# A gated attention and a two-layer network in one kernel: input loads issued six tiles ahead instead of three, and the output pieces of the layer taken one slot later

## The chip, the cores and the metric

The kernel runs on one core of a Trainium2 chip. The metric is device time in microseconds (us) of one launch, the median of several runs. The engines work side by side, each through its own list of instructions in order, and wait for each other by semaphores: PE (TensorE, matrix multiply, with PEld for its weight loads), DVE (VectorE), ACT (ScalarE), POOL (GpSimd) and SP (SyncE, which here only issues DMA transfers).

## The reference

The input is `q`, `k`, `v`, `f_logit`, each of shape (4, 8, 768, 48) in float32, and three weight matrices.

```python
f = 1.0 / (1.0 + np.exp(-f_logit))
for t in range(S):
    state = f[:, :, t, :, None] * state + np.einsum('bhd,bhe->bhde', k[:, :, t], v[:, :, t])
    y[:, :, t] = np.einsum('bhd,bhde->bhe', q[:, :, t], state)
x = y.transpose(0, 2, 1, 3).reshape(B * S, H * D)      # 3072 x 384
out = np.maximum(x @ w1, x @ w2) @ w_out               # d_ff = 1024
```

## The kernel before

The 768 steps of a sequence are cut into 6 chunks of 128, which with the batch of 4 makes 24 tiles of 128 time steps and all 8 heads. Tile n is chunk n // 4 of batch n % 4. Inside a tile the recurrence is done by matrix products, and a small state per batch goes from chunk to chunk. Two tiles make a group g of 256 tokens, for which the layer is computed: the maximum is split as x·w2 + relu(x·(w1 − w2)), so that the layer consists of "d" pieces (the relu part, `piece_d`, four to a group) and "o" pieces (`piece_o`, two to a group, 11 matmuls each, which sum both parts into 128 output rows).

All instructions of an engine stand in the order in which the program's code is run (`manual_schedule`). After a start, in which the weights are loaded and prepared, the loop at the end of the function turns once for each tile; one turn, n, is called slot n here. Its steps stand in this order on every engine they use:

- `load(n + 3)`: four DMAs on SP's queue, for `ft`, `kt`, `qt`, `vt`, 192 KB each, each into one of `bufs=6` buffers of its name.
- A(n): on PE the matmuls into `at_e` and `at_o`, on DVE their masks `at_m`. A slot is taken to begin where PE begins A(n).
- Y(n − 1): on PE `y` and `sadd`, on ACT the copy of `y` into `xT`, on DVE and POOL the new state. Where n is even, ACT also issues two DMAs of 24 KB (`xT<-xT`), which put part of the group's activations into other partitions; the first d piece of the group, in slot n + 1, needs them.
- C(n + 2): on PE `cum`, on ACT the three exponentials `f_inv`, `f_dec`, `f_last`.
- M(n + 2): on POOL `kp` and `qp`.
- one d piece: six matmuls into `h` on PE, one relu into `gT` on ACT.
- V(n + 1) and T(n + 1): on DVE `vb`, on PE transposes into `trp`, on DVE their copy `trs`.
- one d piece.
- E(n + 3): on ACT `tmp_e` from `ft` and then `ell`, which C of the next slot needs.
- one o piece: 11 matmuls into `o` on PE, the copy `ob` on DVE, the store of `ob` on SP's queue.

So SP's queue holds loads and stores in one row, and a load behind a store is issued only when the store's `ob` has been written. Besides, each DMA of SP and of ACT has one of eight semaphores (`DMAHW0` to `DMAHW7`, handed out in turn over both queues), and is issued only when the DMA that had the same one before it has landed.

The pieces stand in one list. The d pieces of group g come into it in slot 2g + 3, and an o piece is not taken as long as a d piece of its group is left; the first o piece of a group follows, in slot 2g + 4, directly on the group's last d piece. The two o pieces of group 0 are there from the start, so slots 2 and 3 have one each, slots 4 and 5 have none, and from slot 6 each slot has one.

Of the kernel before, what the change touches and what calls it, by code (L numbers as in the profile page):

```python
# [16 lines left out]
def kernel(  # L17
# [25 lines left out]
    FG = d_ff // C  # L43
    KT = HD // C
    GB = 2
    NT = GB * C
    n_tiles = nch * B

    consts = ctx.enter_context(tc.tile_pool(name="consts", bufs=1))
    inp = ctx.enter_context(tc.tile_pool(name="inp", bufs=6))  # L50
    work = ctx.enter_context(tc.tile_pool(name="work", bufs=2))
    xpool = ctx.enter_context(tc.tile_pool(name="xpool", bufs=2))
    opool = ctx.enter_context(tc.tile_pool(name="opool", bufs=3))
# [13 lines left out]
    def load(n, names="fkqv"):  # L67
        c, b = divmod(n, B)
        for nm in names:
            t = inp.tile([C, H, D], F32, name=f"{nm}t", tag=f"{nm}t")  # L70
            nc.sync.dma_start(out=t, in_=sources[nm][b, :, c * C:(c + 1) * C, :].rearrange("h p d -> p h d"))  # L71
            loaded[n][nm] = t
# [262 lines left out]
            nc.vector.tensor_copy(m2[:, i, :], ps)  # L335


    AHEAD = 5
    done = set()
    steps = {  # L340
        "E": stage_E, "M": stage_M, "V": stage_V,
# [6 lines left out]
    def do(names, n):  # L348
        for nm in names:
            if 0 <= n < n_tiles and (nm, n) not in done:  # L350
                done.add((nm, n))
                steps[nm](n)
# [5 lines left out]
    load_weights()  # L358
    load(2, "kqv")
    load(3, "kqv")  # L360
    load(4)
    do("E", 0)
    do("E", 1)
    for n in range(2):
# [19 lines left out]
    do("M", 3)  # L384
    do("E", 4)

    queue = [("o", 0, b) for b in range(GB)]

    def next_piece(kind):
        for i, (kd, g, j) in enumerate(queue):  # L390
            if kd == kind:
                if kd == "o" and any(p[0] == "d" and p[1] == g for p in queue):
                    return
                queue.pop(i)
                (piece_d if kind == "d" else piece_o)(g, j)
                return

    n = 2
    while n < n_tiles + 2 or queue:
        if n % GB == 1 and 3 < n <= n_tiles + 1:  # L400
            g = (n - 3) // GB
            queue += [("d", g, fp) for fp in range(FG // 2)] + [("o", g, b) for b in range(GB)]
        if 5 <= n + 3 < n_tiles:
            load(n + 3)
        do("A", n)
        do("Y", n - 1)
        do("C", n + 2)
        do("M", n + 2)
        next_piece("d")
        do("V", n + 1)  # L410
        do("T", n + 1)
        next_piece("d")
        do("E", n + 3)
        next_piece("o")
        n += 1


# [28 lines left out]
```

## Time and profile before

| | us |
|---|---|
| median of 3 runs | 180.33 (179.46 to 181.15) |
| profiled execution, its own time | 179.95 |
| its span, first to last instruction | 178.1 |
| PE busy | 144.2 (81% of the span) |
| ACT busy | 95.4 (54%) |
| DVE busy | 88.8 (50%) |
| POOL busy | 64.1 (36%) |
| DMA queue of SP, share of the 16 engines' span | 76.1% |

The span is the time between the first and the last instruction in one profiled execution; 1.85 us of that execution lie around it. A busy engine need not be the one that everything waits for, since PE's share is an average over a start of some 50 us, in which it waits for weights, the loop, and the last slots.

### The profile page before, as it was taken

What the parts mean: (1) busy time and instruction counts of PE and PEld (TensorE: products, weight loads), DVE (VectorE), ACT (ScalarE), POOL (GpSimd) and SP (SyncE); (2) the same over time, 40 slices, a digit from 0 to 9 for tenths busy, and PEclk for the clock granted to TensorE, in tenths of its full rate; (3) what the DMA queues carried; (4) which work ended last, traced back from release to release, by engine and by line L of the source; (5) the groups of instructions that cost most, each with busy time, mean ns of one, the idle gap of its engine ahead of it and who ended that gap; (6) DMA issues with size and microseconds to landing.
All of it is one profiled execution on the core that took longest, in us unless ns stands there. A gap on an engine that the chain in (4) does not pass through costs nothing.

```text
span 178.1 us, 4161 instructions
## 1 busy us (share of the span) xinstructions
PE 144.2 (81%) x1636; PEld 97.6 (55%) x1637; DVE 88.8 (50%) x168; ACT 95.4 (54%) x205; POOL 64.1 (36%) x79
## 2 busy tenths in 40 slices
PE   0157361877979579999999999999999999999992
PEld 0034250353546457676776757677576775767661
DVE  8029149210289735554666555466554564551121
ACT  4263550385443564866568576684866748343520
POOL 2086009500035181455525445552455524300000
PEclk9999999996999957999999999999999999999999
DMA  6999999990006999689799997999999986111112
GB/s 121 190 228 403 391 261 184 199 157 0 0 4 142 230 196 168 124 172 223 164 225 174 203 186 155 218 188 216 175 189 217 190 167 153 44 53 50 55 48 90
DMA packets 106772, 29.18 MB, mean 164 GB/s; under 512 B 100736, under 2 KB 105984, under 8 KB 106752
## 3 DMA queue, kind: packets, MB, share of 16 engines
q1 hardware_dynamic: 105216, 28.32, 76.1%
q10 hardware_dynamic: 1536, 0.59, 1.3%
q8 instruction: 13, 0.21, 0.5%
q14 instruction: 7, 0.06, 0.1%
HBM read 23.59 MB, written 4.72 MB: 159 GB/s over the span
## 4 chain that ended last, share of the span: by engine, by line
PE 43%; DMA 27%; ACT 10%; DVE 7%; SPq 6%; ACTq 3%; issue 2%; DVEq 0%
DMA ft<-in_f_logit_dram 14%; PE h L275 12%; PE o L285 12%; DMA kt<-in_k_dram 5%; DMA xT<-xT 5%; SPq L71 5%; PE o L282 4%; DMA w_f<-in_moe_w_dram 3%; DVE wdn L305 3%; PE m2n L326 3%; ACTq L265 3%; PE trp L176 2%; PE wdp L312 2%; ACT tmp_e L136 2%; PE y L221 2%
## 5 line engine op out<-in xcount | busy, mean ns | idle before, releaser
L163 POOL TENSOR_TENSOR kp<-kt,f_inv 128x384 bf16<-128x384 f32 x24 | 25.8, 1076 | 51.1 <-ACT f_inv L156 41.0
L275 PE MATMUL h<-xT,wd 128*128 128x256 bf16 x288 | 39.5, 279 | 0.5 <-DMA xT<-xT 0.4
L285 PE MATMUL o<-wo,gT 128*128 128x384 bf16 x192 | 38.0, 327 | 0.5 <-ACT gT L277 0.2
L288 DVE COPY ob<-o 128x384 f32<-128x384 f32 x24 | 13.3, 556 | 45.3 <-PE o L285 41.0
L277 ACT ACTIVATE gT<-h 128x512 bf16<-128x512 f32 x48 | 27.9, 609 | 11.1 <-PE h L275 10.7
L275 PEld LDWEIGHTS <-wd 128*128 128x128 bf16 x288 | 26.4, 99 | 4.2 <-DMA xT<-xT 0.7
L285 PEld LDWEIGHTS <-gT 128*128 128x128 bf16 x192 | 17.3, 98 | 17.3 <-ACT gT L277 7.2
L165 POOL TENSOR_TENSOR qp<-qt,f_dec 128x384 bf16<-128x384 f32 x24 | 24.7, 1031 | 0.3 <-DMA qt<-in_q_dram 0.3
L184 DVE COPY trs<-trp 128x1024 bf16<-128x1024 bf16 x24 | 16.5, 689 | 14.6 <-PE trp L176 14.6
L251 POOL TENSOR_TENSOR state<-tmp_s,f_last 128x256 bf16<-128x256 f32 x16 | 10.6, 662 | 36.5 <-DVE tmp_s L250 36.5
L260 ACT CAST xT<-y 128x512 bf16<-128x512 f32 x24 | 13.9, 581 | 16.9 <-PE y L221 16.9
L136 ACT ACTIVATE tmp_e<-ft 128x384 f32<-128x384 f32 x24 | 12.7, 531 | 16.4 <-DMA ft<-in_f_logit_dram 16.4
L156 ACT ACTIVATE f_inv<-cum 128x384 f32<-128x384 f32 x24 | 11.8, 491 | 16.9 <-POOL state L251 8.4
L143 PE MATMUL cum<-ell,ut 128*128 128x384 bf16 x24 | 8.7, 363 | 11.8 <-ACT ell L137 11.5
L202 DVE TENSOR_TENSOR at_m<-at_e,ut 128x512 bf16<-128x512 f32 x24 | 16.4, 682 | 2.2 <-PE at_o L194 2.1
L202 DVE TENSOR_TENSOR at_m<-at_o,ut 128x512 bf16<-128x512 f32 x24 | 16.3, 680 | 0.0
L282 PE MATMUL o<-m,xT 128*128 128x384 bf16 x72 | 15.6, 326 | 0.0
L169 DVE CAST vb<-vt 128x384 bf16<-128x384 f32 x24 | 11.8, 492 | 2.5 <-DMA vt<-in_v_dram 2.5
L137 ACT ACTIVATE ell<-tmp_e 128x384 bf16<-128x384 f32 x24 | 12.6, 523 | 0.8
L146 PEld LDWEIGHTS <-ell 128*128 128x128 bf16 x96 | 6.1, 100 | 12.3 <-issue 10.9
L194 PE MATMUL at_e<-trs 48*128 48x128 bf16 x96 | 10.1, 229 | 3.2 <-DVE trs L184 3.2
L157 ACT ACTIVATE f_dec<-cum 128x384 f32<-128x384 f32 x24 | 11.7, 488 | 0.0
(51 smaller groups left out, 171.7 us busy)
## 6 DMA issues: line engine op xcount, KB each, us to landing
ft<-in_f_logit_dram SPq DMA_DIRECT2D x24, 192.0 KB, 3.9
kt<-in_k_dram SPq DMA_DIRECT2D x24, 192.0 KB, 4.3
qt<-in_q_dram SPq DMA_DIRECT2D x24, 192.0 KB, 4.2
vt<-in_v_dram SPq DMA_DIRECT2D x24, 192.0 KB, 4.3
out_dram<-ob SPq DMA_DIRECT2D x24, 192.0 KB, 2.4
w_f<-in_moe_w_dram SPq DMA_DIRECT2D x6, 512.0 KB, 6.1
wo_f<-in_moe_w_out_dram SPq DMA_DIRECT2D x2, 768.0 KB, 9.2
xT<-xT ACTq DMA_DIRECT2D x24, 24.0 KB, 3.7
```

The costliest lines, as they stand in the source:

```text
L136: nc.scalar.activation(tmp, ft, AF.Exp, bias=0.0, scale=-1.0)
L137: nc.scalar.activation(padded["ell"][n % NB][:, :, 0:D], tmp.rearrange("p (h d) -> p h d", h=H), AF.Ln, bias=1.0, scale=1.0)
L163: nc.gpsimd.tensor_mul(padded["kp"][n % NB][:, :, 0:D], loaded[n]["k"], f_inv.rearrange("p (h d) -> p h d", h=H))
L165: nc.gpsimd.tensor_mul(padded["qp"][n % NB][:, :, 0:D], loaded[n]["q"], f_dec.rearrange("p (h d) -> p h d", h=H))
L184: nc.vector.tensor_copy(t, ps)
L202: nc.vector.tensor_mul(m[:, r], ps[r], ut4)
L260: nc.scalar.copy(xT[g][:, :, b * C:(b + 1) * C], ys.pop(n))
L275: nc.tensor.matmul(out=ps[:, f, :], lhsT=wd[:, kt, ff * C:(ff + 1) * C], rhs=xT[g][:, kt, :], start=(kt == 0), stop=(kt == KT - 1))
L277: nc.scalar.activation(gT[g][:, 2 * fp:2 * fp + 2, :], ps, AF.Relu)
L282: nc.tensor.matmul(out=ps, lhsT=xT[g][:, kt, b * C:(b + 1) * C], rhs=m2[:, kt, :], start=(kt == 0), stop=False)
L285: nc.tensor.matmul(out=ps, lhsT=gT[g][:, ff, b * C:(b + 1) * C], rhs=wo[:, ff, :], start=False, stop=(ff == FG - 1))
L288: nc.vector.tensor_copy(ob, ps)
```

## The change

There are eight buffers of each input instead of six, `AHEAD` is 6 and is now used: tiles 4 to 7 are loaded before the loop instead of tile 4 alone, and slot n loads tile n + 6 instead of n + 3. The list of pieces becomes two, one for each kind, each entry with the slot from which it may be taken: d pieces of group g from slot 2g + 3 as before, o pieces from slot 2g + 5 instead of 2g + 4. The o pieces of group 0 keep slots 2 and 3.

```diff
-    inp = ctx.enter_context(tc.tile_pool(name="inp", bufs=6))
+    inp = ctx.enter_context(tc.tile_pool(name="inp", bufs=8))
...
-    AHEAD = 5
+    AHEAD = 6
...
-    load(4)
+    for n in range(4, 2 + AHEAD):
+        load(n)
...
-    queue = [("o", 0, b) for b in range(GB)]
-
-    def next_piece(kind):
-        for i, (kd, g, j) in enumerate(queue):
-            if kd == kind:
-                if kd == "o" and any(p[0] == "d" and p[1] == g for p in queue):
-                    return
-                queue.pop(i)
-                (piece_d if kind == "d" else piece_o)(g, j)
-                return
+    queue = {"d": [], "o": [(0, b, 0) for b in range(GB)]}
+
+    def next_piece(kind, slot):
+        if queue[kind] and queue[kind][0][2] <= slot:
+            g, j, _ = queue[kind].pop(0)
+            (piece_d if kind == "d" else piece_o)(g, j)
...
-            queue += [("d", g, fp) for fp in range(FG // 2)] + [("o", g, b) for b in range(GB)]
-        if 5 <= n + 3 < n_tiles:
-            load(n + 3)
+            queue["d"] += [(g, fp, n) for fp in range(FG // 2)]
+            queue["o"] += [(g, b, n + 2) for b in range(GB)]
+        if 2 + AHEAD <= n + AHEAD < n_tiles:
+            load(n + AHEAD)
```

On SP's queue, around the first store, the program before has the load of tile 5 (its last row here is `vt_522`), the store, the load of tile 6 and the second store. The semaphores that a row waits for stand in brackets.

```order
L71 DMA vt_522<-in_v_dram 128x8x48 [waits DMAHW1_49]
L291 DMA out_0_dram<-ob_578 128x384 [waits DMAHW2_49,DVE_49]
L71 DMA ft_581<-in_f_logit_dram 128x8x48 [waits DMAHW3_49,Activation_49]
L71 DMA kt_583<-in_k_dram 128x8x48 [waits DMAHW4_49,Pool_49]
L71 DMA qt_585<-in_q_dram 128x8x48 [waits DMAHW5_49,Pool_49]
L71 DMA vt_587<-in_v_dram 128x8x48 [waits DMAHW6_49]
L291 DMA out_0_dram<-ob_665 128x384 [waits DMAHW0_49,DVE_49]
```

At the same place of SP's queue the changed program has the end of tile 7's load (`vt_201`), all of tile 8's, the store, tile 9's load and the second store.

```order
L71 DMA vt_201<-in_v_dram 128x8x48 [waits DMAHW1_49]
L71 DMA ft_540<-in_f_logit_dram 128x8x48 [waits DMAHW4_49,Activation_49]
L71 DMA kt_542<-in_k_dram 128x8x48 [waits DMAHW5_49,Pool_49]
L71 DMA qt_544<-in_q_dram 128x8x48 [waits DMAHW6_49,Pool_49]
L71 DMA vt_546<-in_v_dram 128x8x48 [waits DMAHW7_49,DVE_49]
L291 DMA out_0_dram<-ob_602 128x384 [waits DMAHW0_49,DVE_49]
L71 DMA ft_605<-in_f_logit_dram 128x8x48 [waits DMAHW1_49,Activation_49]
L71 DMA kt_607<-in_k_dram 128x8x48 [waits DMAHW2_49,Pool_49]
L71 DMA qt_609<-in_q_dram 128x8x48 [waits DMAHW5_49,Pool_49]
L71 DMA vt_611<-in_v_dram 128x8x48 [waits DMAHW6_49]
L291 DMA out_0_dram<-ob_689 128x384 [waits DMAHW7_49,DVE_49]
```

Nine tiles instead of six stand ahead of the first store. `DMAHW2`, for which `kt_607` of tile 9 waits, was last given to the first `xT` DMA of group 1, which ACT issues in slot 4; so SP stops there until that transfer has landed. The later `xT` pairs stop SP in the same way, each once in every two slots, for instance the `vt` of tile 10 (group 2, slot 6), the `ft` of tile 13 (group 3, slot 8) and the fourth store (group 4, slot 10).

On DVE, in slots 5 and 6 (each row of `tmp_s`, `vb`, `trs` and the two of `at_m` is one tile's), the difference is:

```order
 L169 CAST vb_114<-vt 128x8x48
 L184 COPY trs<-trp 128x1024
-L288 COPY ob<-o 128x384
 L202 TENSOR_TENSOR at_m<-at_e,ut_118 128x512
 L202 TENSOR_TENSOR at_m<-at_o,ut_118 128x512
```

Slot 6 loses its o piece; on PE the 11 matmuls of the piece are gone from the same place. At the end of DVE's list the difference is:

```order
 L202 TENSOR_TENSOR at_m<-at_e,ut_118 128x512
 L202 TENSOR_TENSOR at_m<-at_o,ut_118 128x512
-L288 COPY ob<-o 128x384 x5
-L441 UNCONDITIONAL_BRANCH
+L288 COPY ob<-o 128x384 x6
+L439 UNCONDITIONAL_BRANCH
```

The piece stands at the end now, behind the last d pieces; in between, every slot has one o piece as before, but of the group before.

## Rows read from the trace of the kernel before

**Rows 1.** Who waited for whom: us in total, times, longest us.

```profile
ACT tmp_e L136 <- DMA ft<-in_f_logit_dram: 16.4, 13, 3.1
PEld L285 <- ACT gT L277: 7.2, 18, 0.6
```

**Rows 2.** The same for SP's queue.

```profile
SPq L291 <- DVE ob L288: 63.6, 23, 16.8
...
SPq L71 <- DMA xT<-xT: 7.6, 2, 7.1
```

**Rows 3.** Stretches: us, busy PE, PEld, DVE, ACT, POOL, PEclk, DMA share, GB/s.

```profile
62.50:68.50 6.00, 4.88 (x39) 3.40 (x40) 2.15 (x5) 3.62 (x9) 3.73 (x5) 0.50 1.18 185
74.00:148.00 74.00, 72.76 (x944) 50.90 (x944) 42.32 (x84) 48.15 (x111) 35.86 (x42) 1.00 0.95 189
```

**Rows 4.** PE in order of time, slots 4 to 7: start, us, what, [idle before].

```profile
57.65 0.41 PE L221 MATMUL y<-at_m,vb 128*64 128x128 bf16 x8
...
63.50 0.48 PE L143 MATMUL cum<-ell,ut 128*128 128x384 bf16 x1 [1.35 <-ACT ell L137]
...
64.18 1.46 PE L275 MATMUL h<-xT,wd 128*128 128x256 bf16 x6
...
67.70 0.28 PE L194 MATMUL at_e<-trs 48*128 48x128 bf16 x1
...
75.02 0.81 PE L275 MATMUL h<-xT,wd 128*128 128x256 bf16 x6
```

**Rows 5.** ACT in order of time, slots 3 and 4.

```profile
58.16 0.52 ACT L136 ACTIVATE tmp_e<-ft 128x384 f32<-128x384 f32 x1 [2.34 <-DMA ft<-in_f_logit_dram]
...
59.15 0.57 ACT L260 CAST xT<-y 128x512 bf16<-128x512 f32 x1
59.75 1.23 ACTq L265 DMA_DIRECT2D xT<-xT  x2
```

**Rows 6.** ACT in order of time in slot 10.

```profile
90.35 0.58 ACT L260 CAST xT<-y 128x512 bf16<-128x512 f32 x1 [0.28 <-PE y L221]
90.96 1.21 ACTq L265 DMA_DIRECT2D xT<-xT  x2
...
93.08 1.11 ACT L277 ACTIVATE gT<-h 128x512 bf16<-128x512 f32 x2
...
94.62 0.52 ACT L137 ACTIVATE ell<-tmp_e 128x384 bf16<-128x384 f32 x1
```

**Rows 7.** PE in order of time: slots 8, 9 and 10, and A of 22.

```profile
78.66 0.23 PE L194 MATMUL at_e<-trs 48*128 48x128 bf16 x1
...
84.17 0.23 PE L194 MATMUL at_e<-trs 48*128 48x128 bf16 x1
...
85.58 0.81 PE L275 MATMUL h<-xT,wd 128*128 128x256 bf16 x6
...
87.34 0.65 PE L282 MATMUL o<-m,xT 128*128 128x384 bf16 x3
87.83 1.46 PE L285 MATMUL o<-wo,gT 128*128 128x384 bf16 x8
89.22 0.23 PE L194 MATMUL at_e<-trs 48*128 48x128 bf16 x1
...
92.88 1.86 PE L285 MATMUL o<-wo,gT 128*128 128x384 bf16 x8
...
153.56 0.23 PE L194 MATMUL at_e<-trs 48*128 48x128 bf16 x1
```

**Rows 8.** The xT DMAs' time to landing: all 24, slots 8, 18 and 22.

```profile
DMA to landing us min/median/max: 1.9/3.7/5.8
...
DMA to landing us min/median/max: 3.1/3.3/3.5
...
DMA to landing us min/median/max: 3.5/4.3/5.0
...
DMA to landing us min/median/max: 1.9/1.9/1.9
```

More of the change, by code (lines that the diff above doesn't have):

```diff
@@ L385 @@
     do("E", 4)
-    queue = [("o", 0, b) for b in range(GB)]
-    def next_piece(kind):
-        for i, (kd, g, j) in enumerate(queue):
-            if kd == kind:
-                if kd == "o" and any(p[0] == "d" and p[1] == g for p in queue):
-                    return
-                queue.pop(i)
-                (piece_d if kind == "d" else piece_o)(g, j)
-                return
+    queue = {"d": [], "o": [(0, b, 0) for b in range(GB)]}
[3 more added lines that the diff above has]
+            (piece_d if kind == "d" else piece_o)(g, j)
     n = 2
-    while n < n_tiles + 2 or queue:
+    while n < n_tiles + 2 or queue["d"] or queue["o"]:
         if n % GB == 1 and 3 < n <= n_tiles + 1:
             g = (n - 3) // GB
-            queue += [("d", g, fp) for fp in range(FG // 2)] + [("o", g, b) for b in range(GB)]
-        if 5 <= n + 3 < n_tiles:
-            load(n + 3)
+            queue["d"] += [(g, fp, n) for fp in range(FG // 2)]
+            queue["o"] += [(g, b, n + 2) for b in range(GB)]
+        if 2 + AHEAD <= n + AHEAD < n_tiles:
+            load(n + AHEAD)
         do("A", n)
@@ L408 @@
         do("M", n + 2)
-        next_piece("d")
+        next_piece("d", n)
         do("V", n + 1)
         do("T", n + 1)
-        next_piece("d")
+        next_piece("d", n)
         do("E", n + 3)
-        next_piece("o")
+        next_piece("o", n)
         n += 1
```

## The prediction

> **What bounds the kernel now.** I read the waits first, because the change names its target: loads that come late. ACT waits 16.4 us in total for `ft`, 13 times [rows 1], and SP stands 63.6 us in front of stores whose `ob` is not there yet [rows 2]. That looks like much to win. The second view, the stretches, says otherwise: between 74 and 148 us PE is busy for 72.76 of 74.00 us at full clock [rows 3], so nearly all of ACT's waiting there is covered by PE's work, and only what PE itself loses can come back. So the third view is PE in order of time, slot by slot.
>
> In the loop, slot 9 lasts from 84.17 to 89.22, 5.05 us, and the eight matmuls on `gT` take 1.46 us in it; slot 10 begins at 89.22, and there the same eight take 1.86 [rows 7]. In the even slots the o piece follows directly on the last d piece of its own group and waits some 0.4 us for the relu, which ACT does late because it issues two DMAs in the same slot [rows 6]. That is the wait of PE's weight loads for `gT`, 18 times and 7.2 us [rows 1] (as seen by the loads, which overlap the matmuls, so it isn't all lost). From A(8) at 78.66 to A(22) at 153.56 are 14 slots and 74.90 us [rows 7]; at 5.05 us each it would be 70.70. **PE loses 4.2 us in the loop**, whatever the cause.
>
> Before that, slots 4 to 7 aren't bound by PE. In slot 4 ACT waits 2.34 us for `ft` of tile 6 [rows 5]; behind it in ACT's queue stand the copy into `xT` (59.15) and the two `xT` DMAs, though its input `y` was done at 58.06 [rows 4]. The first d piece of group 1 begins at 64.18, when they have landed. PE idles so much that its clock falls: from 62.5 to 68.5 the granted clock is 0.50 (1.2 GHz) [rows 3].
>
> **The loads, slots 4 and 5.** Nine tiles are ahead of the first store, so tile 6's `ft` is there long before E(6), and slot 4's copy goes at about 58.1 instead of 59.15. What is late next on this way: C(7) needs `ell` of tile 7. From copy to the end of `ell`, ACT takes 94.62 + 0.52 − 90.35 = 4.8 us in slot 10, with two relus of about 1.0 together between them [rows 6]; slot 4 has no d piece, so 3.8: 61.9, and C takes some 0.35 (half of 64.18 − 63.50 [rows 4], which was at half clock). The other input is the `xT` pair: the second one is issued 1.2 us behind the start of the copy, at 59.3, and lands 1.9 us (no loads in flight) to 3.8 us later (near the median, 3.7) [rows 8], at 61.2 to 63.1. SP has just stopped in front of tile 9's `kt`, which waits for this very transfer, so few loads are in flight; I take the low end. d(1,0) then begins at 62.4 instead of 64.18. The upper end would give 63.1.
>
> **The clock.** PE still idles in slots 4 and 5 (slot 4 holds no piece at all), so I let the clock fall as before, and take the 3.5 us from d(1,0) to A(6), 64.18 to 67.70 [rows 4], as they are: A(6) at 65.9.
>
> **The o piece, slots 6 and 7.** An o piece takes 89.22 − 87.34 = 1.9 us of PE [rows 7]. Slot 6 gets shorter by it on PE (3.2 us left), but ACT has the same work as in slot 10: the copy begins 1.1 us behind A [rows 6, 7] (1.4 at the low clock), `ell` is done 4.8 us later, then C(9): d(2,0) at 65.9 + 1.4 + 4.8 + 0.35 = 72.45, before 75.02 [rows 4]. **Gained up to there: 2.6 us.** The piece itself comes back at the end, where PE has nothing else: **plus 1.9 us.** So the front, which the loads are for, is worth 0.7 net.
>
> **The loop from slot 8.** Here the loads change little and the later o piece much: its `gT` is a slot old, so the 0.4 us of the even slots go. The rest of the 4.2 us are `ft` waits that reach PE and waits for `xT`. **Minus 4.2 us**, if all go. What comes in their place is the `xT` pair, since the slot between its issue and its use gets shorter. The second DMA is issued about 2.35 us behind A (91.55 against 89.22) [rows 6, 7]; d begins at A + 5.05 + 1.41 (85.58 − 84.17) [rows 7]: it may take 4.1 us to land. Under loads it takes 3.1 to 5.0 us (slots 8 and 18 are the best and the worst pair there), without them 1.9 [rows 8]. Bounds: nothing, or 0.9 us a pair. The last load is issued around slot 18 now, so six pairs, of slots 8 to 18, are under loads: 0 to 5.3 us. The best pair lies under the limit, the worst 0.9 over it, the median of all 24 is 3.7; I take 0.2 a pair, **plus 1.2 us**.
>
> ACT in an even slot, 5.9 us from A to the end of `ell` [rows 6, 7], still ends before C of the next slot, which begins 0.35 ahead of d, at 6.1. SP's stops at the `xT` pairs hold back its stores and loads by up to two slots; `ft` of tile 10 would go at about 64 and is read in slot 7, after 75, so this has cover of some 7 us, and of a slot or more later. Eight buffers cost nothing that a row shows. What stands ahead of slot 4 keeps its order.
>
> **Sum:** −2.6 + 1.9 − 4.2 + 1.2 = −3.7 us. The profiled execution took 179.95, so 176.25; the median of the runs is 0.4 above it, so **176.6 us**.
>
> **The rivals.** (1) *The clock stays up in slots 5 and 6.* For it: the change takes idle time out of slot 4. Against it: much of the idle time there, PE behind DVE and ACT, stays. PE was busy 4.88 us at half clock [rows 3]; at full clock this is 2.4 less, of which I keep 2.0 for the waits that would show: 174.6.
>
> (2) *The clock falls a second time.* Taking the o piece out of slot 6 makes PE wait for ACT some 2 us in slot 7, on top of the idle slots 4 and 5, where just such a state brought it down. Then d, T, d and o of slot 7, 3.6 us of PE work (5.05 − 1.41 [rows 7]), run partly at half clock, 0 to 3.6 more, I take 1.7: 178.3. The Trainium skill, TensorE: Matmul & The Clock Gate, section "HAM oscillation — how this bites in real kernels", says that waits between bursts of matmuls put the clock back to half, so that each burst starts cold again. By that rule this case is the likelier one, against the rows from 74 us on, where the clock holds.
>
> (3) *The xT wait takes the place of the gT wait, and more.* Its place is the first d piece of every odd slot, its price 6 × (landing − 4.1). From a landing of 4.9 us in every pair the gain is gone, from 5.25 the kernel is slower by 1%; at 5.8, the longest of the trace [rows 8], it is −4.9 + 10.2: 185.3. For it: loads are now never short of a queue in slots 8 to 18. Against it: they were dense already, a DMA share of 0.95 [rows 3], and SP now stops until the pair has landed. The Trainium skill, DMA: Bandwidth & Descriptors, section "Issuing engines are not separate DMA queues", has ACT's and SP's transfers interleave on the same 16 engines, which speaks for this rival; the 1.9 against 3.1 to 5.0 us agree with it.
>
> (4) *The loads don't run ahead.* SP's stops at the `xT` pairs keep them as late as the stores did, ACT waits for `ft` in slot 4 as before, and only the moved piece counts: the 2.6 shrink to nothing, 179.2.
>
> **How the numbers follow.** Forecast 0.44, clock up 0.17, second fall 0.20, xT 0.07, loads no earlier 0.12. About 1% (1.8 us) is what a measurement of this kernel can tell from no change, so faster means under 178.5. Faster: nearly all of the forecast, all of (1), half of (2), a quarter of (4), 0.73; slower: most of (3) and a little of each, 0.06; the rest, 0.21, is within 1%. The range reaches from (1) with no `xT` wait at all (173.6) to just above (4): 173.8 to 179.4; outside are most of (3) and the ends of (1) and (2).
>
> **What would show it.** ACT's wait for `ft` at `tmp_e` near zero; d(1,0) near 62.4 and d(2,0) near 72.5; the eight `gT` matmuls 1.46 us in even slots too; slots of 5.05 us, longer only where PE waits for `xT`; no loads after some 137 us; two o pieces at the end with no d between them. I am wrong if even slots stay at 5.4 us with a new wait, if the clock is at 0.50 beyond 69 us, or if ACT, not PE, sets the odd slots too.

## The result, and the profile after

The changed kernel takes 174.91 us (174.69 to 175.49, four runs); the kernel before takes 180.56 (179.46 to 181.15, four runs). The ratio is 0.9699, 95% interval 0.9645 to 0.9752. Ratios, here and below, leave out runs in a slower state, so that they can differ a little from those of the medians. The profiled execution took 174.97 with a span of 173.1, which is 5.0 less than the 178.1 of before.

First the waits of the changed kernel (us in total, times, longest us), beside [rows 1]:

```profile
PE cum L143 <- ACT ell L137: 10.6, 5, 4.7
...
ACT tmp_e L136 <- DMA ft<-in_f_logit_dram: 6.4, 3, 3.4
...
PE at_e L194 <- DVE trs L184: 3.7, 5, 1.3
```

ACT's wait for `ft` went from 16.4 us in 13 times to 6.4 in 3, and these three lie in the start. PE's weight loads wait nowhere for `gT` any more. What PE still waits for is `ell` and `trs`, in the slots before 76 us.

SP's queue, beside [rows 2]:

```profile
SPq L291 <- DVE ob L288: 36.6, 15, 5.9
SPq L71 <- DMA xT<-xT: 19.6, 9, 7.0
...
SPq L291 <- DMA xT<-xT: 4.4, 3, 1.9
```

SP stands less in front of stores, and more in front of loads whose semaphore an `xT` DMA still holds. That costs nothing that the profile shows: behind the start ACT waits for no `ft`.

The stretches (us, busy PE, PEld, DVE, ACT, POOL, clock, DMA share, GB/s), beside [rows 3]:

```profile
62.50:68.50 6.00, 5.07 (x93) 4.15 (x89) 4.49 (x9) 4.94 (x13) 4.73 (x6) 1.00 0.83 172
74.00:140.00 66.00, 65.95 (x887) 48.47 (x886) 39.59 (x79) 43.70 (x102) 32.94 (x39) 1.00 0.99 197
```

In the loop PE is busy for 65.95 of 66.00 us. Between 62.5 and 68.5, where the granted clock was 0.50 before, it is 1.00 in this execution.

PE in order of time (start, us, what, [idle before]), beside [rows 4] and [rows 7]:

```profile
63.62 0.32 PE L143 MATMUL cum<-ell,ut 128*128 128x384 bf16 x1 [0.49 <-ACT ell L137]
...
63.88 0.82 PE L275 MATMUL h<-xT,wd 128*128 128x256 bf16 x6
...
65.93 0.23 PE L194 MATMUL at_e<-trs 48*128 48x128 bf16 x1
...
72.14 0.32 PE L143 MATMUL cum<-ell,ut 128*128 128x384 bf16 x1 [1.17 <-ACT ell L137]
...
72.41 0.81 PE L275 MATMUL h<-xT,wd 128*128 128x256 bf16 x6
...
76.04 0.23 PE L194 MATMUL at_e<-trs 48*128 48x128 bf16 x1
...
86.33 0.23 PE L194 MATMUL at_e<-trs 48*128 48x128 bf16 x1
...
89.98 1.46 PE L285 MATMUL o<-wo,gT 128*128 128x384 bf16 x8
91.38 0.23 PE L194 MATMUL at_e<-trs 48*128 48x128 bf16 x1
```

Slot 10 (86.33 to 91.38) is even, and its eight matmuls on `gT` take 1.46 us instead of 1.86, the slot 5.05 instead of 5.46. Of the waits that the change leaves in slots 4 to 7, those of 0.49 and 1.17 us are for `ell`; the longest is 1.29 us for `trs`, in front of A(5).

The landing of the `xT` DMAs issued around 87 and 97 us, beside [rows 8]:

```profile
DMA to landing us min/median/max: 3.9/4.0/4.2
...
DMA to landing us min/median/max: 3.5/3.7/4.0
```

**Where the 5.0 us come from.** The span falls into four stretches at A(2), A(8) and A(22), each read from PE in order of time:

| stretch, us | before | after | difference |
|---|---|---|---|
| to A(2) | 50.30 | 51.93 | +1.63 |
| A(2) to A(8), the front | 28.36 | 24.11 | −4.25 |
| A(8) to A(22), 14 slots of the loop | 74.90 | 70.87 | −4.03 |
| A(22) to the end | 24.54 | 26.19 | +1.65 |

The first stretch got longer although its code on PE is the same. Ten matmuls that prepare the weights carry most of it; here of the kernel before:

```profile
32.92 3.22 PE L312 MATMUL wdp<-wdn,perm 128*128 128x512 bf16 x10 [0.22 <-issue]
```

and of the changed one:

```profile
33.00 4.45 PE L312 MATMUL wdp<-wdn,perm 128*128 128x512 bf16 x10 [0.22 <-issue]
```

Nothing is waited for between them; they run more slowly for longer. The granted clock reads 1.00 over this stretch in both profiles, which doesn't explain it. In e6 and e8 (below), whose starts are nearly as long (51.88 and 51.48 us), it reads 0.50 from 30 to 36 us. So a clock that rises late is a likely cause, not a shown one.

### The profile page after: what moved, and what is told of

It reads as the page before. It is cut to its first block, busy times and chain, and to the rows that moved or that the text cites. A ratio compares the mean times of both kernels' runs of the same rounds, so it can differ in the third digit from the quotient of the medians.

```text
span 173.1 us, 4159 instructions
## 1 busy us (share of the span) xinstructions
PE 140.5 (81%) x1636; PEld 97.8 (56%) x1637; DVE 88.4 (51%) x168; ACT 94.4 (55%) x205; POOL 64.4 (37%) x79
## 4 chain that ended last, share of the span: by engine, by line
PE 66%; DMA 9%; DVE 8%; ACT 6%; SPq 6%; issue 2%; ACTq 1%
PE h L275 18%; PE o L285 17%; PE o L282 6%; DMA kt<-in_k_dram 5%; SPq L71 5%; PE trp L176 4%; PE at_e L194 4%; PE y L221 4%; PE y L216 3%; DMA w_f<-in_moe_w_dram 3%; PE wdp L312 3%; PE m2n L326 3%; DVE wdn L305 3%; PE cum L143 3%; ACT wo L322 2%
## 5 line engine op out<-in xcount | busy, mean ns | idle before, releaser
L275 PE MATMUL h<-xT,wd 128*128 128x256 bf16 x288 | 38.1, 272 | 0.1
L285 PE MATMUL o<-wo,gT 128*128 128x384 bf16 x192 | 35.1, 326 | 0.0
L275 PEld LDWEIGHTS <-wd 128*128 128x128 bf16 x288 | 25.9, 98 | 3.9 <-issue 1.0
L285 PEld LDWEIGHTS <-gT 128*128 128x128 bf16 x192 | 18.8, 98 | 12.4
L202 DVE TENSOR_TENSOR at_m<-at_e,ut 128x512 bf16<-128x512 f32 x24 | 16.4, 682 | 2.0 <-PE at_o L194 2.0
L136 ACT ACTIVATE tmp_e<-ft 128x384 f32<-128x384 f32 x24 | 12.8, 532 | 6.4 <-DMA ft<-in_f_logit_dram 6.4
L194 PEld LDWEIGHTS <-trs 48*128 48x128 bf16 x192 | 5.7, 97 | 11.2 <-DVE trs L184 5.9
```

The lines of the kernel that those rows point to most:

```text
L194: nc.tensor.matmul(out=ps[r][:, j, :], lhsT=t[rows, 0, j, :], rhs=t[rows, 1, j, :], start=True, stop=True)
L202: nc.vector.tensor_mul(m[:, r], ps[r], ut4)
L275: nc.tensor.matmul(out=ps[:, f, :], lhsT=wd[:, kt, ff * C:(ff + 1) * C], rhs=xT[g][:, kt, :], start=(kt == 0), stop=(kt == KT - 1))
L285: nc.tensor.matmul(out=ps, lhsT=gT[g][:, ff, b * C:(b + 1) * C], rhs=wo[:, ff, :], start=False, stop=(ff == FG - 1))
```

## The experiments

The same four stretches for every profile told below (of e7 only the times are used); slots 4 to 7 are lengths from A to the next A:

| kernel | to A(2) | front | loop | end | slots 4, 5, 6, 7 | median us | ratio to before, interval |
|---|---|---|---|---|---|---|---|
| before | 50.30 | 28.36 | 74.90 | 24.54 | 3.63 6.75 5.91 5.05 | 180.56 | |
| after | 51.93 | 24.11 | 70.87 | 26.19 | 2.98 4.00 3.84 6.27 | 174.91 | 0.9699 (0.9645–0.9752) |
| e12, after again | 51.60 | 25.36 | 70.76 | 26.18 | 2.98 5.04 4.03 6.28 | 175.86 | 0.9705 (0.9635–0.9775) |
| e1, loads alone | 51.09 | 26.40 | 75.13 | 24.48 | 2.97 5.46 5.89 5.05 | 178.25 | 0.9841 (0.9788–0.9894) |
| e2, later o alone | 50.46 | 28.21 | 72.31 | 26.22 | 3.85 7.01 4.03 6.29 | 180.22 | 0.9943 (0.9888–0.9998) |
| e3, after with 4 ahead | 51.23 | 26.28 | 71.15 | 26.24 | 2.97 5.97 4.03 6.28 | 175.76 | 0.9638 (0.9580–0.9696) |
| e7, loads alone, 4 ahead | | | | | | 179.29 | 0.9854 (0.9815–0.9893) |
| e4, before with filler | 50.83 | 27.02 | 75.04 | 24.51 | 3.81 5.45 5.69 5.05 | 179.82 | 0.9941 (0.9903–0.9979) |
| e5, later xT in code | 50.21 | 25.05 | 71.53 | 26.21 | 2.98 5.42 4.03 5.59 | 174.94 | 0.9654 (0.9612–0.9696) |
| e11, xT behind relu | 51.80 | 24.42 | 72.64 | 26.44 | 2.97 4.02 3.83 6.57 | 177.04 | 0.9753 (0.9690–0.9817) |
| e6, hole in slot 7 | 51.88 | 24.68 | 71.60 | 26.24 | 2.97 5.33 5.89 3.46 | 175.15 | 0.9652 (0.9600–0.9704) |
| e8, e6 with filler | 51.48 | 23.17 | 71.68 | 26.17 | 2.98 4.00 5.69 3.47 | 173.57 | 0.9576 (0.9516–0.9635) |
| e9, e5 with filler | 50.44 | 23.94 | 70.62 | 26.30 | 2.98 4.00 3.84 6.09 | 174.61 | 0.9620 (0.9544–0.9697) |
| e10, e5, e6 and filler | 50.20 | 22.90 | 70.99 | 26.21 | 2.97 4.01 5.42 3.47 | 173.24 | 0.9547 (0.9479–0.9614) |

The ratios of e1 to e12 are against runs of the kernel before on the same chip; the kernel before took 181.15 us beside e1 to e4, 181.64 beside e5 to e8, and 181.24 beside e9 to e12.

**The two halves of the change.** e1 is the kernel before with the loads alone (eight buffers, six ahead):

```diff
-    inp = ctx.enter_context(tc.tile_pool(name="inp", bufs=6))
+    inp = ctx.enter_context(tc.tile_pool(name="inp", bufs=8))
-    load(4)
+    for n in range(4, 2 + AHEAD):   # AHEAD = 6
+        load(n)
-        if 5 <= n + 3 < n_tiles:
-            load(n + 3)
+        if 2 + AHEAD <= n + AHEAD < n_tiles:
+            load(n + AHEAD)
```

> Only the loads: eight buffers, six tiles ahead, o pieces as before. Theory A (the loads are worth slots 4 to 7, with the clock that stays up there, and little in the loop): from A(2) to d(1,0) about 12.0 us instead of 13.9, clock at 1.00 from 57 us on, then slot 6 with its o piece; the even slots keep the 0.4 us for gT, so A(8) to A(22) 73 to 74 us; in all 176 to 177.5. Theory B (the loop's whole gain is that ft no longer holds ACT, and the later o piece only costs its 1.9 us at the end): even slots 5.05 us, about 173.

e2 is the changed kernel with the old loads, so that only the o pieces come later:

```diff
-    inp = ctx.enter_context(tc.tile_pool(name="inp", bufs=8))
+    inp = ctx.enter_context(tc.tile_pool(name="inp", bufs=6))
-    AHEAD = 6
+    AHEAD = 3
```

> Only the later o piece: six buffers, three tiles ahead as before. Theory A: A(8) to A(22) falls from 74.9 to 71 to 72 us, the end gets 1.7 longer, slots 4 and 5 stay as they are with ACT's wait for ft and the clock at 0.50 behind it; slot 6 is shorter by up to 1; in all 178 to 179.5. Theory B: the loop keeps its 74 us or more and the end costs 1.9, so 181 to 182.5.

e1 gains 1.6%, e2 0.6%, both together 3.0%. In the stretches the halves hardly overlap: the loads shorten the front (28.36 to 26.40) and not the loop (74.90 to 75.13), the later pieces shorten the loop (to 72.31) and not the front (28.21), and pay 1.7 us at the end. The loop of the changed kernel, 70.87, is below both. Theory B of either run is out: e1's even slots in the loop take 5.45 us and more, not 5.05, and e2's loop did not keep its 74 us. But neither time lies in the range of its theory A. e1's 178.25 us are above 176 to 177.5, as its clock fell (0.50 from 64 to 66 us) and its loop is longer than 73 to 74; e2's 180.22 lie between its two ranges, with a loop of 72.31 for 71 to 72. Here are e1's waits:

```profile
PEld L285 <- ACT gT L277: 8.7, 18, 1.6
ACT tmp_e L136 <- DMA ft<-in_f_logit_dram: 6.4, 3, 3.2
ACT f_inv L156 <- DMA xT<-xT: 2.5, 1, 2.5
```

and e2's:

```profile
ACT tmp_e L136 <- DMA ft<-in_f_logit_dram: 15.8, 10, 3.4
```

e1 has rid ACT of the `ft` waits, as the changed kernel has, and still its loop is as long as before, since the wait for `gT` is there 18 times. So in the loop of the kernel before, the `ft` waits were mostly covered by PE's work.

e2's loop is 1.44 us longer than that of the changed kernel, by PE waits of two kinds:

```profile
100.52 0.32 PE L143 MATMUL cum<-ell,ut 128*128 128x384 bf16 x1 [0.35 <-ACT ell L137]
...
147.33 0.83 PE L275 MATMUL h<-xT,wd 128*128 128x256 bf16 x6 [0.81 <-DMA xT<-xT]
```

The first is an `ell` that comes late because ACT stood 1.52 us for `ft`; slots 12 and 14 together are 0.6 us longer by such waits. The second is in slot 21, which takes 5.90 us, and 4.92 in the changed kernel. Its `xT` pair lands in 3.7 and 4.9 us, beside loads that e2 issues until 144.5 us; the changed kernel issues its last load at 135.79, and its pair of the same group lands in 2.4 and 3.2 us. So of what the loads add to the loop of e2, 0.6 us are `ft` waits that the later pieces had uncovered, and 1.0 is the room of an `xT` pair, because the loads are over earlier; 0.2 go off for a wait of the changed kernel in slot 9 (see below).

e1 also pays where nothing was expected, in slot 20, which takes 6.57 us for 5.46 before. ACT in order of time there:

```profile
142.86 2.33 ACTq L265 DMA_DIRECT2D xT<-xT  x2
145.29 0.49 ACT L156 ACTIVATE f_inv<-cum 128x384 f32<-128x384 f32 x1 [2.46 <-DMA xT<-xT]
```

and PE:

```profile
146.77 0.99 PE L285 MATMUL o<-wo,gT 128*128 128x384 bf16 x4 [1.19 <-ACT gT L277]
```

The pair of issues, 1.21 us elsewhere [rows 6], takes 2.33. In the program the second `xT` DMA here signals the same semaphore as a store of SP's queue ahead of it. That does not explain it, for this store was issued at 132.52 us, and its landing view says

```profile
DMA to landing us min/median/max: 5.5/5.5/5.5
```

so it had landed at 138.0, 4.9 us before the pair was issued. Nor do the deep loads: e4 below, with the loads of the kernel before, shows the same in slot 20, which takes 6.28 us. Its pair takes 2.04 us, where that of the kernel before itself takes 1.21:

```profile
143.42 2.04 ACTq L265 DMA_DIRECT2D xT<-xT  x2
```

What lengthens the issue stays open. Without the 1.1 us of slot 20 e1's loop would be 74.0 us, at the upper end of theory A's range.

**How deep the loads must be.** e3 is the changed kernel with six buffers and four tiles ahead; e7 the same depth on the kernel before, without the later pieces.

```diff
-    inp = ctx.enter_context(tc.tile_pool(name="inp", bufs=8))
+    inp = ctx.enter_context(tc.tile_pool(name="inp", bufs=6))
-    AHEAD = 6
+    AHEAD = 4
```

> Six buffers and loads four tiles ahead instead of six (tiles 4 and 5 ahead of the loop, tile 6 in slot 2 ahead of the first store), o pieces late. If all that the loads need is that ft of tiles 6 and 7 is not behind a store whose ob is late: E(6) and E(7) in time, the time of the changed kernel within 0.7 us, 174.5 to 175.5. If the depth itself matters (bursts that overrun, loads that arrive late in the loop): ft waits at tmp_e again, and 176 or more.

> Six buffers, loads four tiles ahead, o pieces as before (the loads' part alone, in the shallow form). If the shallow form is all that slots 4 to 7 need, and the deep loads of the run with loads alone cost it something through the stores that come late in SP's queue and the semaphore that a store shares with an xT DMA: no even slot over 5.8 us, and 177 to 178, a little under the deep form's 178.25. If the depth matters: 179 or more.

e3 is as fast as the changed kernel (0.9638 against 0.9699 and 0.9705, the intervals overlap), with the same 6.4 us of `ft` waits, and e7 (0.9854) as fast as e1 (0.9841). In us, e3's 175.76 lie between its two ranges, and e7's 179.29 in the range for a depth that matters; but the kernel before is slower beside e7 than beside e1, so the ratios count. By the times, one tile more ahead of the loop, and one more in it, is all that the depth is worth. The profile of e3 shows one thing more, at d(1,0):

```profile
64.10 1.44 PE L275 MATMUL h<-xT,wd 128*128 128x256 bf16 x6 [0.70 <-DMA xT<-xT]
```

d(1,0) begins 12.87 us behind A(2), where the changed kernel has 11.95 and e12, the same kernel once more, 11.96; slot 5 takes 5.97 us, and 5.04 in e12, though the clock falls in both. The `xT` pair lands in 3.4 and 3.7 us in e3, at a DMA share of 1.17 from 58 to 62 us, and in 1.9 and 2.0 in the changed kernel and in e12, at 0.11 and 0.05. With six tiles ahead SP stands there in front of tile 9's `kt`, which waits for this very pair; with four it issues loads. So the greater depth gives 0.9 us in slot 5, which the times can't tell from nothing.

**The clock.** e4 is the kernel before with four matmuls of 512 columns more in slots 4 and 5, between Y and C, whose result nobody reads:

```diff
+        if n in (4, 5):
+            filler(4)      # 4 x matmul(out=bank("fill"), lhsT=ident, rhs=w2b[:, 0, 0:512])
         do("C", n + 2)
```

> The kernel before with four extra 512-column matmuls (0.9 us, their result is not read) on PE in slots 4 and 5, where it idles behind Y. If the fall of the clock at 62 us comes from these idle stretches: clock at 1.00 there, d(1,0) where it was, A(6) about 1.5 us earlier, 178.5 to 179.5 in all. If the fall has nothing to do with them: clock 0.50 as before and 180 to 181.

Its stretches are

```profile
56.00:62.00 6.00, 4.58 (x60) 2.67 (x59) 4.84 (x9) 2.06 (x6) 2.05 (x2) 1.00 1.03 210
62.00:70.00 8.00, 6.69 (x106) 5.08 (x106) 5.05 (x9) 5.80 (x14) 5.21 (x6) 1.00 1.07 179
```

so the clock holds at 1.00 (2.4 GHz) with more work on PE, and slot 5 takes 5.45 us instead of 6.75. The mean granted clock over the span was 0.988 to 0.990 in all six runs of e4, and 0.950 to 0.981 in eleven runs of the kernel before. The front is 1.3 us shorter and the time 0.6%, less than the 2.4 us that 4.88 busy us at half clock [rows 3] would give back if nothing else were waited for; here the `xT` pair is, at d(1,0), and 179.82 us lie just above the range of the first case:

```profile
65.04 0.83 PE L275 MATMUL h<-xT,wd 128*128 128x256 bf16 x6 [0.78 <-DMA xT<-xT]
```

e12 is the changed kernel once more, beside e9, e10 and e11:

> The changed kernel once more, beside the others on the same chip. The start differs by the time at which the clock rises there (A(2) at 50.2 to 51.9 us in the runs so far), and slots 5 and 6 by whether it falls: 174 to 176.

Here the clock did fall:

```profile
62.00:64.00 2.00, 1.51 (x36) 1.29 (x34) 1.96 (x4) 1.89 (x6) 2.00 (x3) 1.00 0.50 100
64.00:66.00 2.00, 2.00 (x16) 1.67 (x14) 0.61 (x2) 1.23 (x4) 2.00 (x3) 0.51 1.26 230
66.00:68.00 2.00, 2.00 (x36) 1.24 (x34) 0.88 (x3) 1.21 (x3) 0.47 (x1) 0.64 0.74 166
68.00:70.00 2.00, 1.80 (x32) 1.62 (x27) 1.25 (x4) 0.79 (x2) 0.66 (x1) 1.00 0.79 157
```

with slot 5 at 5.04 us instead of 4.00 and a front of 25.36 instead of 24.11. One program, two courses: after PE's idle time in slots 4 and 5 the clock falls in e12, e1, e3, e5 and e6, and not in the first profile of the changed kernel or in e11. In the changed kernel it is a matter of the execution, worth 1.0 us in slot 5 and 1.25 in the front. The mean clock over the span, 0.990 in the first profile and 0.978 in that of e12, hints at how often: three of the first four runs have 0.99, and none of e12's four is above 0.980.

**The limit of the xT pair.** Two kernels issue the pair of groups from 2 on later. e5 moves it in ACT's list from behind the copy to behind the three exponentials of C:

```diff
         if b == GB - 1:
-            x = xT[g]      # and the two dma_start
+            if g > 1:
+                late.append(g)
+            else:
+                move_xT(g)
...
         do("C", n + 2)
+        while late:
+            move_xT(late.pop())   # the two dma_start
```

> The changed kernel, with the xT DMAs of groups 2 and later issued about 1.0 us later, behind the three exponentials of C on ACT. If the first d piece of an odd slot has only the 4.1 us that were worked out between the second DMA's issue and its start: pairs that land in 3.6 to 4.2 us now make PE wait 0.5 to 1.1 us, in slots 9, 11, 13, 15, 17 and perhaps 19, none in 21 and 23 where landing takes 1.9; A(8) to A(22) 74 to 77 us instead of 70.9, in all 178 to 181. If the pair has slack (the limit is not there): no change, 174.9.

The later issue did not come. ACT in e5, in slot 10:

```profile
86.49 0.59 ACT L268 CAST xT<-y 128x512 bf16<-128x512 f32 x1 [1.24 <-PE y L221]
87.02 0.49 ACT L156 ACTIVATE f_inv<-cum 128x384 f32<-128x384 f32 x1
87.16 0.56 ACTq L262 DMA_DIRECT2D xT<-xT  x1
87.40 0.48 ACT L157 ACTIVATE f_dec<-cum 128x384 f32<-128x384 f32 x1
87.76 0.60 ACTq L262 DMA_DIRECT2D xT<-xT  x1
```

The issue begins at 87.16, 0.67 us behind the start of the copy, beside the first exponential; in the changed kernel it begins 0.62 behind it. The activations ahead of it in the list run meanwhile, and only those behind it wait. So e5 delays nothing and instead takes the issues out of ACT's way; the time stays (174.94), and its loop is 71.53 us here and 70.62 in e9, which has the same order. e11 puts the pair behind the first relu, whose input comes from PE:

```diff
         next_piece("d", n)
+        while late:
+            move_xT(late.pop())
         do("V", n + 1)
```

> The changed kernel, with the xT DMAs of groups 2 and later issued on ACT behind the first relu of the even slot: the second one then goes about 3.1 us behind A instead of 2.35, and has 3.4 us to land. If the limit is real (landing 3.6 to 4.2 us under loads, 1.9 to 2.8 behind them): PE waits 0.2 to 0.8 us at the first d piece in slots 9 to 19, none in 21 and 23; A(8) to A(22) 72.5 to 75 us, 176.5 to 179 in all. If not: 71 us and 174.9.

Its second DMA of slot 14 is issued at 110.47, 2.93 us behind A (2.35 in [rows 6, 7]), and PE then waits:

```profile
107.54 0.23 PE L194 MATMUL at_e<-trs 48*128 48x128 bf16 x1
...
112.59 0.23 PE L194 MATMUL at_e<-trs 48*128 48x128 bf16 x1
...
114.48 0.81 PE L283 MATMUL h<-xT,wd 128*128 128x256 bf16 x6 [0.33 <-DMA xT<-xT]
```

The landing view of the same pair says

```profile
DMA to landing us min/median/max: 3.7/3.8/3.9
```

So the second DMA lands at 114.4 at the latest, where d could otherwise begin at 112.59 + 1.41 = 114.00. The six odd slots under loads are 5.22 to 5.56 us, 2.0 more in all than six of 5.05, and the loop is 72.64 against 70.76 of e12 on the same chip. So 0.6 us less room brings the wait, and the changed kernel stands just in front of it. The medians, 177.04 and 175.86, agree with this, though the intervals of the two ratios overlap.

**The idle time of slot 7.** With the later pieces slot 6 has no o piece and PE waits 1.17 us in slot 7. e6 gives the first o piece of group 1 back to slot 6 and leaves slot 7 without one; e8 is e6 with two filler matmuls in slots 4 and 5 (as in e4); e9 is e5 with the filler; e10 has all three.

```diff
-            queue["o"] += [(g, b, n + 2) for b in range(GB)]
+            queue["o"] += [(g, b, n + 2 if g > 1 else n + 1 + 2 * b) for b in range(GB)]
```

> The changed kernel with the slot that has no o piece moved from 6 to 7: o(1,0) in slot 6 with its wait for gT, o(1,1) in slot 8, then as before. If ACT's 5 us of work in an even slot is what PE waits for in slots 6 and 7 when the piece is gone, an odd slot (ACT 3.8 us) is the better place for the hole: about 1 us less, 173.5 to 174.5. If the idle time in slots 6 and 7 comes from elsewhere (the late ell of slots 4 and 5): the same 174.9, or up to 0.5 more by the wait for gT.

> The version with the hole in slot 7, and two extra 512-column matmuls in slots 4 and 5, whose result is not read. If the clock still falls in some runs without them: mean clock 0.99 in every run and a narrower spread, 173 to 174.5 (0 to 1 us under the one without). If the clock stays up there anyway: the same time as without, or up to 0.4 more.

> The changed kernel with the xT DMAs behind the exponentials (as in the run that did that alone: ACT is done 0.8 us earlier in an even slot, the transfer goes only 0.1 us later) and two extra 512-column matmuls in slots 4 and 5. If the extra matmuls keep the clock up in slots 5 and 6: mean clock 0.99 in all runs, slot 7 at 5.6 us instead of 6.3, 172.8 to 174. If the xT waits of slots 15 to 19 eat what ACT gains: 174.5 to 175.

> The same with the slot without an o piece moved from 6 to 7. If what the two places of the hole differ in is ACT's time in an even slot: with ACT 0.8 us shorter there the difference shrinks from 0.6 to nothing, so equal to the run beside it within 0.4 us. If the hole in an odd slot is better by itself: 0.6 less, 172.3 to 173.4.

Slots 6 to 8 add up to 5.89 + 3.46 + 5.42 = 14.77 us in e6, and to 4.03 + 6.28 + 5.06 = 15.37 in e12, both with a falling clock. That is 0.6 less for the forecast 1, and the ratio of e6 (0.9652 against 0.9699 and 0.9705) can't tell it from nothing. With the filler slot 5 takes 4.0 us in e8, e9 and e10, and no profile of them shows a fall in slots 4 to 7. The mean clock of 0.99 in every run, which was expected, did not come: two of e8's four runs have 0.97, and one each of e9 and e10. The profile of e8 is one of these; there the clock is at 0.50 from 30 to 36 us, in the start.

e9 is no faster than e5 beyond its interval. Its slot 7 takes 6.09 us, not 5.6, and the rival's `xT` waits did not come either. Slots 6 to 8 add up to 14.31 us in e10 and 14.98 in e9, so that the hole in the odd slot is worth about as much with ACT's shorter even slots (0.67) as without (0.6). That speaks against ACT's time as what the two places differ in, with one profile each. e10 is the fastest kernel of the study, 173.24 us, 2.6 below the changed kernel on the same chip (175.86). Between the two profiles the whole gain lies in front of A(8), 73.10 us against 76.96, and 1.4 of it are the start, which differs from run to run. PE in e10 from slot 5 on:

```profile
60.20 0.23 PE L194 MATMUL at_e<-trs 48*128 48x128 bf16 x1 [0.86 <-DVE trs L184]
...
61.34 0.60 PE L401 MATMUL fill<-w2b,ident 128*128 128x512 bf16 x2
...
62.16 0.82 PE L283 MATMUL h<-xT,wd 128*128 128x256 bf16 x6
...
73.10 0.23 PE L194 MATMUL at_e<-trs 48*128 48x128 bf16 x1
```

## Why the prediction was right, and where its terms were off

The time fell by 3.0%, where 2.2% had been forecast, and 174.91 lies in the range. By its steps:

- **The loads, slots 4 and 5: right.** From A(2) to d(1,0) the forecast was 62.4 − 50.30 = 12.1 us; it is 63.88 − 51.93 = 11.95 in the profile after and 11.97 in e1. The low end of the landing had been taken because SP stops there; e3, in which it does not, has 12.87, where the upper end was 63.1 − 50.30 = 12.8. That ACT's 16.4 us of waiting for `ft` were mostly covered is shown by e1, which removes 10.0 of them and keeps the loop's length.
- **The clock: the wrong course for the profiled execution, the right one for others.** The forecast let it fall and kept 3.5 us from d(1,0) to A(6); it took 2.05, as rival (1) has it. In e12 it fell and took 66.65 − 63.56 = 3.1. That A(6) stands at 65.93 where 65.9 was written is luck, two errors that cancel: 1.6 us more in the start, 1.5 less here. The 2.0 that rival (1) kept for a clock that stays up was too much: 1.25 between the two fronts of the changed kernel, 1.3 between those of before and e4.
- **The o piece: right.** d(2,0) comes 20.48 us behind A(2) (21.73 in e12), where 22.15 was forecast and 24.72 was the case before; most of the rest is the clock. At the end 1.65 to 1.7 us come back (after, e2) for the forecast 1.9.
- **The loop: right, for a reason that has two parts.** 4.2 us were to go; 4.03 did, with the new waits already taken off. e2 shows that the later pieces are worth 2.6 of it; the other 1.4 need the loads as well, 0.6 by `ft` in time and 1.0 by the `xT` pair of slot 20, which lands faster when the loads are over, less 0.2 in slot 9.
- **The new xT wait: the term that was mis-sized.** 1.2 us were set, 0.2 for each of six pairs. Of the six only that of slot 8 makes PE wait, 0.19 us in slot 9, where it lands in 3.7 and 4.2 us. (Slot 17 is 0.08 longer too, but its pair, at most 3.9 us under way, had landed at 122.9, and d began at 123.19.) The loop is 70.87 where slots without any wait make 13 × 5.05 + 4.92 = 70.57. The limit of 4.1 us was right, as e11 shows; the spread of the landings was not. It had been taken from the pairs of before, 3.1 to 5.0; in slots 8 to 18 those of the changed kernel land in 3.5 to 4.2. So rival (3) has a real place and a real price, which e2 pays in slot 21, but the deeper loads do not lengthen the landing beyond that of before. The Trainium skill, DMA: Bandwidth & Descriptors, section "Issuing engines are not separate DMA queues", lets ACT's and SP's transfers interleave on the same engines. The landings agree, 3.5 to 4.2 under loads against 1.9 without [rows 8].
- **Rival (2), a second fall of the clock,** came in none of the runs that were profiled: from 72 us on the granted clock is 1.00 in all of them, although PE idles 1.17 us in slot 7. The Trainium skill, TensorE: Matmul & The Clock Gate, section "HAM oscillation — how this bites in real kernels", has each burst behind a wait start cold again, in a kernel whose waits are longer than its bursts. Slots 4 to 6 of e12 agree with it: from 60 to 62 us PE was busy for 0.71 of 2.00 us, and from 64 to 66 the clock is at 0.51. In slot 7 the wait, 2 us in the forecast and 1.17 in the trace, is shorter than the 3.6 us of work behind it, so this rule did not make the rival the likelier case, as the prediction has it.
- **Rival (4)** is out: the last load is issued at 135.79 us, and ACT waits for `ft` nowhere in the loop.

Three small sums of the prediction are off, without consequence: 61.9 + 0.35 is 62.25 and not 62.4, rival (1) without an `xT` wait is 174.6 − 1.2 = 173.4 and not 173.6, and the 185.3 of rival (3) lacks the 0.4 us between the profiled execution and the median that the other times have.

With a start as before (−1.63) the span would have shrunk by 6.6 instead of 5.0; with the fall of the clock by some 5.4. Why the start is longer in this execution stays open. A(2) lies between 50.20 and 51.93 in thirteen profiles, at 50.30 to 50.83 in the three with the old loads (before, e2, e4) and at 50.20 to 51.93 in the ten with the new ones. e10 and e5 have the new loads and the shortest starts, so the loads don't force it; whether they make it likelier was not tried.

## What to carry to other kernels

A wait of an engine that is not the bottleneck says little about what its removal brings: follow it to the slot in which the bottleneck itself idles, and expect its worth to change when the next wait there goes. Where two waits end close together, removing one can show little, as the loads alone did in the loop, so test them apart and together before dropping either. A transfer's landing depends on what else is in flight, 1.9 us against 3.4 to 3.7 for the same pair here, so look at what the other queue does at that time. Before a transfer's consumer is moved earlier, work out how long the transfer may take, since here 0.6 us less room turned a hidden landing into a wait in every second slot.

## What the hardware showed that was not expected

- An issue of a DMA in ACT's list goes on beside the activations that stand ahead of it (e5: issue at 87.16, exponentials from 87.02 to 87.9), while the activations behind it wait for it (1.34 us at `f_inv` in the changed kernel's slot 4, put down to the issue).
- The same pair of issues took 2.33 us instead of 1.21 in e1 and 2.04 in e4, and in e1 ACT stood 2.46 us. The DMA that had the semaphore before had landed 4.9 us ahead of the pair in e1, so it isn't that; the cause is open.
- A load of SP that waited for the `xT` pair kept the DMA engines nearly idle while the pair was under way: 1.9 and 2.0 us at a DMA share of 0.11 in the changed kernel, 3.4 and 3.7 at 1.17 in e3, where SP did not stop.
- The granted clock at the same place of the same program differs from one execution to the next: 1.00 and 0.51 around 65 us in two profiles of the changed kernel. With two small matmuls more in each of the two idle slots it stayed at 1.00 there in all three kernels that had them, one profile each.
- Ten equal matmuls at 33 us took 3.22 us in one execution and 4.45 in another, with no wait between them.
